# An attention and FFN kernel on Trainium2: v pieces and w3 loads in another order, one product in the short chunk

## Chip, core and metric

The kernel runs on one core of a Trainium2 chip. The metric is device time in microseconds (us) of one execution. Five runs of the kernel before gave a median of 572.65 us (571.81 to 573.43). A core has five engines with a queue of instructions each: TensorE (PE in the profile, with PEld for its weight loads), VectorE (DVE), ScalarE (ACT), GpSimd (POOL) and SyncE (SP). They run side by side and wait for each other through semaphores; each queue runs in order. SP issues the stores of the output and the transposes by DMA, POOL issues the loads.

## What is computed

```python
B, N, C = (4, 5824, 256)
qn = q / (np.linalg.norm(q, axis=1, keepdims=True) + 1e-06)
kn = k / (np.linalg.norm(k, axis=1, keepdims=True) + 1e-06)
s = kn.transpose(0, 2, 1) @ qn / tau
s = s - s.max(-1, keepdims=True)
a = np.exp(s)
a /= a.sum(-1, keepdims=True) + 1e-09
x = (v @ a).reshape(B * N, C)
out = ((x @ w1) * (x @ w2) @ w3) @ w_out     # w1, w2: 256 x 1024, w3: 1024 x 1024, w_out: 1024 x 256
```

All inputs and the output are float32. The attention is over the 256 columns (a is 256 x 256 for each of the 4 batches), then an FFN multiplies two projections and projects the product back.

## The kernel before

**Folding.** For each batch the 256 x 256 matrix a is multiplied into w1 and w2 first, which gives `Wf` (the folds, L342 to L387). Also w3 and w_out are multiplied once, into `W_sb` (`w_unit`, L624). What is left for each row block is `a = vT x Wf[0]`, `b = vT x Wf[1]`, their product, and that times `W_sb`.

**Tiling.** A batch has 5824 rows: 45 groups of 128 and 64 left over. `v` is loaded in six pieces of up to eight groups (`PIECE`), cast to bf16 on the way, and transposed into `vT` (slots of 128 rows) and, for the last full group with the 64 left over, `vTt`. A chunk is four slots, 512 columns; there are eleven of them and a short chunk of 128 + 64 columns (`NCH` is 12). A piece serves two chunks: piece 1 serves chunks 2 and 3, piece 3 chunks 6 and 7. Pieces, chunks and batches are counted from 0 in all that follows; the fourth and fifth v piece are pieces 3 and 4.

**The main loop** (L694) goes over batches, chunks and eight blocks j of 128 columns of F. `emit_ab` (L457) issues two products for `a` and two for `b`, a copy of `a` to SBUF on ACT (L469) and the product with `b` on DVE (L478; for the short chunk L480, and L483 for the 64 left over). The result waits in the list `pend`; `emit_out` (L488) multiplies it with `W_sb` and, at j = 7, copies the finished tile (ACT L524, DVE L525) and stores it (SP L526). `LAG` results are kept waiting; until `W_sb` is ready none is taken out, and afterwards up to two at each step. The 64 rows left over of an even and the following odd batch make up one 128-row product together (`lefts`).

**What sets the order.** The program is issued in a written order, not by a scheduler. `make_agenda` (L644) fills a list of due times on a running count of the time that PE's products should take (`clock`); `run_due` issues what is due between the steps of the main loop. On the agenda stand the loads of the next pieces (`moves`), their transposes 4 later, the score products of the next batch (`score_units`, between `t0` and `t1`) and its softmax and folds (`soft_units`).

**Queues.** POOL's queue holds the loads, and what stops them from starting early: `gate` (L448, a copy of one element that waits for the latest product) and `hold` (L453, a copy of one element that waits for the transposed piece before). The all-reduce of the norms (L258) is in the same queue. SP's queue holds the transposes by DMA and the output's stores.

**The start.** Batch 0's q and k come first, then v piece 0, w1 and w2, v pieces 1 and 2, w_out and w3 (L601, L602). Piece 0 and piece 1 are transposed on PE in halves (`transpose_half_on_pe`), piece 2 and all that follow by DMA on SP. w3 is transposed by four DMAs (L553) into buffers of k's pool; `w_unit` then makes `W_sb` in eight parts, each of eight products. Batch 0's sums of the exponentials (L328) are taken by products with a column of ones; DVE adds 1e-9 and takes the reciprocal `rs` (L334, L335), by which the folds are scaled.

Of the kernel before, what the change touches and what calls it, by code (L numbers as in the profile page):

```python
# [12 lines left out]
F32 = DT.float32  # L13
BF16 = DT.bfloat16

P = 128
PIECE = 8
LAG = 2
IN_BUFS = {"q": 5, "k": 6, "v": 3}
MM_COL = 1.0 / 2400.0  # L20
MM_FIX = 0.0025
# [3 lines left out]
def kernel(  # L25
# [52 lines left out]
    nc.vector.memset(warm, 0.0)  # L78
    ones_pp = consts.tile([P, P], F32)
    nc.vector.memset(ones_pp, 1.0)  # L80
    eps_t = consts.tile([P, 1], F32)
    nc.vector.memset(eps_t, 1e-6)

# [65 lines left out]
    def transpose_piece(n, pi):  # L149
        if pi == 0:  # L150
            new_vT(n)
        vT, vTt = vTs[n]
        t = pieces.pop(("v", n, pi))
        if pi < NP_ - 1:
            nc.sync.dma_start_transpose(vT[:, pi * PIECE : (pi + 1) * PIECE, :, :], t[:, :, :])
        else:
            g = LAST - 1
            nc.sync.dma_start_transpose(vT[:, pi * PIECE : pi * PIECE + g, :, :], t[:, :g, :])
            nc.sync.dma_start_transpose(vTt[:, :, :P], t[:, g, :])
            nc.sync.dma_start_transpose(vTt[:, :, P:], t[:LEFT, g + 1, :])  # L160


    G_tiles = {}
# [75 lines left out]
    def soft_units(n):  # L239
# [75 lines left out]
        def exps(ct):  # L315
# [3 lines left out]
                out=st["e"][:, ct, :], in_=st["s"][:, ct, :], func=AF.Exp, scale=st["r"][:, ct : ct + 1]  # L319
            )  # L320

        def sum_mm(c2):
            if c2 == 0:
                st["sum"] = psum.tile([P, 512], F32, tag="out" if n == 0 else "G", name=f"sum_{n}", bufs=3 if n == 0 else 1)
                Wf[n] = wf_pool.tile([P, CT, 2, F], BF16, tag="Wf", name=f"Wf_{n}")
            m = st["sum"]
            for c1 in range(CT):
                nc.tensor.matmul(  # L328
                    m[:, c1 : c1 + 1], lhsT=st["e"][:, c2, c1 * P : (c1 + 1) * P], rhs=ones_b,
                    start=(c1 == 0 and c2 == 0), stop=(c1 == CT - 1 and c2 == CT - 1), skip_group_check=True,  # L330
                )
            if c2 == CT - 1:
                rs = work.tile([P, CT], F32, tag="rs", name=f"rs_{n}", bufs=2)
                nc.vector.tensor_scalar_add(rs, m[:, :CT], 1e-9)  # L334
                nc.vector.reciprocal(rs, rs)  # L335
                st["rs"] = rs

        def sums():
# [61 lines left out]
                    quarter_mm(256, c1, c2)  # L400

        if n == 0:
            return [k_first, k_row, q_first, scaled_first, first_folds, second_quarter] + [lambda i=i: fold(i) for i in range(4, 8)]

        return (
            [(0.0, 0.0, norms), (0.0, 6.0, k_row)]
# [50 lines left out]
    def emit_ab(b, c, j):  # L457
        n = chunk_cols(c)
        tiles = []
        for w in range(2):  # L460
            t = psum.tile([P, 512], F32, tag="ab", name=f"{'ab'[w]}_{b}_{c}_{j}", bufs=4)
            for ct in range(CT):
                nc.tensor.matmul(  # L463
                    t[:, :n], lhsT=Wf[b][:, ct, w, j * P : (j + 1) * P], rhs=rhs_of(b, c, ct),
                    start=(ct == 0), stop=(ct == CT - 1),
                )
# [3 lines left out]
        if b == 0 and c < 2:  # L470

            if j % 4 == 0:
                held[0] = in_pool.tile([P, 4, 512], BF16, tag="q", name=f"abq_{c}_{j}", bufs=IN_BUFS["q"])
            ab = held[0][:, j % 4, :]
        else:
            ab = work.tile([P, 512], BF16, tag="ab_sb", name=f"abs_{b}_{c}_{j}", bufs=8 * NDEF + 6)
        if n == 4 * P:
            nc.vector.tensor_mul(ab, a_sb, tiles[1])  # L478
        else:
            nc.vector.tensor_mul(ab[:, :P], a_sb[:, :P], tiles[1][:, :P])  # L480
            if b % 2 == 0 and j == 0:
                lefts[b // 2] = work.tile([P, FT, 2, LEFT], BF16, tag="left", name=f"left_{b}", bufs=1)
            nc.vector.tensor_mul(lefts[b // 2][:, j, b % 2, :], a_sb[:, P:n], tiles[1][:, P:n])  # L483
        pend.append((b, c, j, ab))
        last_ab[0] = ab
        clock[0] += 4 * (n * MM_COL + MM_FIX)

    def emit_out(b, c, j, ab):  # L488
        small = c == NCH - 1
        if small:  # L490
            lhs = [ab[:, :P]]
            if b % 2 == 1:
                lhs.append(lefts[b // 2][:, j, :, :].rearrange("p b t -> p (b t)"))
        else:
            lhs = [ab[:, i * P : (i + 1) * P] for i in range(4)]
        if j == 0:
# [2 lines left out]
                for h in range(len(lhs) if small else 2)  # L499
            ]  # L500
        tl = out_tiles[b, c]
        for s, lhsT in enumerate(lhs):
            h, o = (s, 0) if small else divmod(s, 2)
            nc.tensor.matmul(  # L504
                tl[h][:, o, :], lhsT=lhsT, rhs=W_sb[:, j, :],
                start=(j == 0 and o == 0), stop=(j == FT - 1 and (small or o == 1)),
                skip_group_check=True,
            )
# [89 lines left out]
    load_part("v", 0, 0, half, PIECE)  # L598
    load_piece("v", 0, 1)
    load_piece("v", 0, 2)  # L600
    nc.gpsimd.dma_start(out=wout_sb, in_=moe_w_out.rearrange("(lh ll) c -> ll lh c", ll=P))  # L601
    nc.gpsimd.dma_start(out=w3_bf, in_=w3r)  # L602
    squares("k", 4, whole)
    for sl in (lo, hi):
        squares("q", 4, sl)
# [4 lines left out]
    for i, sl in enumerate(parts):  # L610
# [5 lines left out]
        if i == 0:  # L616
            soft0[1]()
    soft0[3]()
    busy(3)
    transpose_half_on_pe(0, 0, 0, False)  # L620
    soft0[4]()
    w_ready = [False]

    def w_unit(jt):  # L624
        m = psum.tile([P, 512], F32, tag="ab", name=f"w_{jt}", bufs=4)
        for lt in range(FT):
            nc.tensor.matmul(  # L627
                m[:, :D], lhsT=w3T[jt // 2][:, jt % 2, lt, :], rhs=wout_sb[:, lt, :],
                start=(lt == 0), stop=(lt == FT - 1),
            )  # L630
        if jt % 2 == 0:
            nc.scalar.copy(W_sb[:, jt, :], m[:, :D])
        else:
            nc.vector.tensor_copy(W_sb[:, jt, :], m[:, :D])
        if jt == FT - 1:
            w_ready[0] = True

    def load_library():

# [4 lines left out]
    def make_agenda(b):  # L644
# [3 lines left out]
        if b == 0:  # L648
            at(0.5, 0.87, soft0[5])
            for i in range(4):  # L650
                at((1.7, 2.6, 3.5, 3.9)[i], 0.43, soft0[6 + i])
# [38 lines left out]
        for i, (cst, t, fn) in enumerate(soft):  # L690
            at(t1 + 1.0 + t + (2.0 if b == 0 and i > 0 else 0.0), cst, fn)
        agenda.sort()

    for b in range(B):  # L694
        make_agenda(b)
        for c in range(NCH):
            for j in range(FT):
                run_due()
                emit_ab(b, c, j)
                npop = 0  # L700
                while w_ready[0] and len(pend) > LAG and npop < 2:
                    emit_out(*pend.pop(0))
                    npop += 1
                    run_due()
# [38 lines left out]
```

## Time and profile before

| What | us |
|---|---|
| median of five runs | 572.65 (571.81 to 573.43) |
| the profiled execution | 573.43 |
| its span, first to last instruction | 571.4 |
| first a product on PE | 37.94 |
| w_out issued, us to landing | 36.3, 15.1 |
| w3 issued, us to landing | 37.2, 24.0 |
| first and last w product on PE | 65.4, 76.1 |
| PE's longest wait after the start, for w3T | 0.71 |
| last PE product ends | 567.73 |

The span is the time from the first to the last instruction; the profiled execution's own time holds 2.0 us more around it. A line of a timeline gives start and duration in us, engine, source line, operation and tiles, `out<-in`, and in brackets the idle time ahead with what ended it. In a line of waits the numbers are the total, the count and the longest. In the lines of the DMA issues the last number is the time from the issue to the landing. The granted clock of TensorE was 1.00 throughout the work.

### The profile page before, as it was taken

What the parts mean: (1) busy time and instruction counts of PE and PEld (TensorE: products, weight loads), DVE (VectorE), ACT (ScalarE), POOL (GpSimd) and SP (SyncE); (2) the same over time, 40 slices, a digit from 0 to 9 for tenths busy, and PEclk for the clock granted to TensorE, in tenths of its full rate; (3) what the DMA queues carried; (4) which work ended last, traced back from release to release, by engine and by line L of the source; (5) the groups of instructions that cost most, each with busy time, mean ns of one, the idle gap of its engine ahead of it and who ended that gap; (6) DMA issues with size and microseconds to landing.
All of it is one profiled execution on the core that took longest, in us unless ns stands there. A gap on an engine that the chain in (4) does not pass through costs nothing.

```text
span 571.4 us, 10131 instructions
## 1 busy us (share of the span) xinstructions
PE 558.4 (98%) x3753; PEld 354.8 (62%) x3753; DVE 377.5 (66%) x613; ACT 339.7 (59%) x627; POOL 78.3 (14%) x164
## 2 busy tenths in 40 slices
PE   7789999999999999999999999999999999999997
PEld 5664567776655666666666666666665666666665
DVE  1047645788967567888767567787877656565564
ACT  1047535778756577777665577777765554454454
POOL 4260012112030110120220011021120000000000
PEclk9999999999999999999999999999999999999999
DMA  9999988897674596686761595856750325221011
GB/s 211 212 168 209 158 164 203 206 207 173 149 170 103 101 216 147 114 157 153 148 148 46 122 199 134 154 119 125 178 117 38 84 73 148 63 63 75 38 68 61
DMA packets 75104, 77.45 MB, mean 136 GB/s; under 512 B 54192, under 2 KB 58800, under 8 KB 75056
## 3 DMA queue, kind: packets, MB, share of 16 engines
q0 software_dynamic: 15760, 38.93, 39.4%
q1 hardware_dynamic: 59072, 37.69, 21.6%
q8 instruction: 29, 0.48, 0.3%
q10 hardware_dynamic: 224, 0.20, 0.1%
q14 instruction: 19, 0.16, 0.1%
HBM read 78.91 MB, written 23.86 MB: 180 GB/s over the span
## 4 chain that ended last, share of the span: by engine, by line
PE 91%; DMA 6%; ACT 1%; DVE 1%; issue 0%; POOL 0%; ACTq 0%; POOLq 0%
PE o L504 27%; PE a L463 27%; PE b L463 27%; PE G L188 5%; DMA k<-in_k_dram 5%; PE fold L350 2%; DMA w3T<-w_wout 1%; PE w L627 1%; ACT as L469 1%; PE quarter L376 0%; ACT kr L279 0%; POOL k L109 0%; DVE s L313 0%; ACT e L318 0%; DVE abs L478 0%
## 5 line engine op out<-in xcount | busy, mean ns | idle before, releaser
L478 DVE TENSOR_TENSOR abs<-as,b 128x512 bf16<-128x512 bf16 x336 | 230.0, 686 | 140.3 <-ACT as L469 127.8
L469 ACT CAST as<-a 128x512 bf16<-128x512 f32 (+1 forms) x384 | 215.9, 563 | 172.7 <-DVE abs L478 85.0
L463 PEld LDWEIGHTS <-Wf 128*128 128x128 bf16 x1536 | 149.0, 98 | 102.8 <-issue 2.3
L463 PE MATMUL a<-vT,Wf 128*128 128x512 bf16 x704 | 209.4, 379 | 0.8 <-DVE Wf L387 0.6
L504 PE MATMUL o<-W_sb,abs 128*128 128x256 bf16 x1376 | 209.9, 273 | 0.1
L463 PE MATMUL b<-vT,Wf 128*128 128x512 bf16 x704 | 209.3, 379 | 0.0
L504 PEld LDWEIGHTS <-abs 128*128 128x128 bf16 x1376 | 134.5, 98 | 81.9 <-DVE abs L480 0.3
L197 DVE TENSOR_TENSOR acc<-acc,sq 128x1024 f32<-128x1024 f32 x66 | 80.4, 1218 | 0.4 <-ACT sq L185 0.4
L188 PE MATMUL G<-k,q 128*128 128x256 bf16 x276 | 49.6, 273 | 0.0
L185 ACT ACTIVATE sq<-q 128x512 f32<-128x512 bf16 x66 | 41.8, 634 | 0.0
L185 ACT ACTIVATE sq<-k 128x512 f32<-128x512 bf16 x66 | 41.5, 629 | 0.0
L451 POOL COPY gate_t<-abs 1x1 bf16<-1x1 bf16 x39 | 10.5, 269 | 170.9 <-DVE abs L478 170.0
L525 DVE COPY osb<-o 128x512 f32<-128x512 f32 x44 | 30.1, 683 | 0.8 <-PE o L504 0.7
L188 PEld LDWEIGHTS <-q 128*128 128x128 bf16 x276 | 27.0, 98 | 3.1
L524 ACT COPY osb<-o 128x512 f32<-128x512 f32 x44 | 25.8, 586 | 3.8 <-PE o L504 1.8
L455 POOL COPY gate_t<-vT 1x1 bf16<-1x1 bf16 x17 | 3.3, 195 | 178.1 <-DMA vT<-v 178.1
L109 POOL DMA_DIRECT2D q<-in_q_dram x28 | 15.2, 541 | 13.1 <-DMA k<-in_k_dram 5.5
L279 ACT ACTIVATE kr<-row 128x256 f32<-128x256 f32 x1 | 0.4, 384 | 26.2 <-PE row L267 26.2
L357 ACT ACTIVATE Wf<-fold,rs 128x512 bf16<-128x512 f32 x15 | 10.3, 688 | 8.9 <-PE fold L350 7.7
L350 PE MATMUL fold<-w,e 128*128 128x512 bf16 x56 | 15.0, 379 | 0.2 <-ACT as L469 0.2
L478 DVE TENSOR_TENSOR abq<-as,b 128x512 bf16<-128x512 bf16 x16 | 10.8, 686 | 5.2 <-ACT as L469 4.6
L109 POOL DMA_DIRECT2D k<-in_k_dram x24 | 13.6, 566 | 4.1 <-DMA k<-in_k_dram 3.3
(95 smaller groups left out, 234.3 us busy)
## 6 DMA issues: line engine op xcount, KB each, us to landing
out_dram<-osb SPq DMA_DIRECT2D x44, 512.0 KB, 3.1
k<-in_k_dram POOLq DMA_DIRECT2D x19, 512.0 KB, 8.6
v<-in_v_dram POOLq DMA_DIRECT2D x19, 512.0 KB, 5.3
q<-in_q_dram POOLq DMA_DIRECT2D x18, 512.0 KB, 5.8
w_wout<-in_moe_w_dram POOLq DMA_DIRECT2D x1, 2048.0 KB, 24.0
k<-in_k_dram POOLq DMA_DIRECT2D x4, 320.0 KB, 5.9
v<-in_v_dram POOLq DMA_DIRECT2D x4, 320.0 KB, 5.2
q<-in_q_dram POOLq DMA_DIRECT2D x3, 320.0 KB, 4.3
```

What stands on the lines that cost most here:

```text
L109: nc.gpsimd.dma_start(out=pieces[nm, n, pi][:, lo:hi, :], in_=qk_main[nm, n][0][:, pi * PIECE + lo : pi * PIECE + hi, :])
L185: nc.scalar.activation(out=dst[:, :, part, :], in_=src[:, o : o + 2, :], func=AF.Square)
L188: nc.tensor.matmul(G[:, ct, :], lhsT=qt[:, i, ct * P : (ct + 1) * P], rhs=kt[:, i, :], start=(pr == 0 and part == 0 and ct == 0), stop=(pr ...
L197: nc.vector.tensor_add(accs[n], accs[n], sqs[0])
L350: nc.tensor.matmul(m, lhsT=st["e"][:, c2, c1 * P : (c1 + 1) * P], rhs=w12[:, c2, w, lo:hi], start=(c2 == 0), stop=(c2 == CT - 1),)
L451: nc.gpsimd.tensor_copy(gate_t, last_ab[0][:1, :1])
L463: nc.tensor.matmul(t[:, :n], lhsT=Wf[b][:, ct, w, j * P : (j + 1) * P], rhs=rhs_of(b, c, ct), start=(ct == 0), stop=(ct == CT - 1),)
L469: nc.scalar.copy(a_sb[:, :n], tiles[0][:, :n])
L478: nc.vector.tensor_mul(ab, a_sb, tiles[1])
L504: nc.tensor.matmul(tl[h][:, o, :], lhsT=lhsT, rhs=W_sb[:, j, :], start=(j == 0 and o == 0), stop=(j == FT - 1 and (small or o == 1)), skip ...
L524: nc.scalar.copy(o[:, 0:2, :], tl[0])
L525: nc.vector.tensor_copy(o[:, 2:4, :], tl[1])
```

## The change

Seven edits, all in the kernel's order and tiles:

- The second v piece (piece 1) of batch 0 is transposed by DMA on SP instead of on PE; pieces 2 and 1, in this order, are transposed before w3.
- w_out and w3 are loaded by POOL only when piece 1 has been transposed (`load_w3` behind a `hold`).
- The parts of `W_sb` are due from 35.0 instead of 26.0, in PSUM tiles of the tag `out` instead of `ab`.
- Batch 0's moves have other times. The first hold waits for the last w3T tile; v pieces 3 and 4 are loaded one behind the other without a hold between, and transposed one behind the other.
- In the short chunk DVE makes one product of 192 columns. The 64 left over lie behind the 128 for an even batch and ahead of them for an odd one, so that the two parts of 64 stand side by side.
- For batch 0 the 1e-9 comes from a product with the constant `tiny` that opens the sums' accumulation; DVE's add falls away.
- `LAG_END` keeps five results waiting in the last chunk; the softmax of batch 1 is no longer due 2.0 later than in the other batches.

```diff
+LAG_END = 5
@@
+    tiny = consts.tile([1, P], F32)
+    nc.vector.memset(tiny, 1e-9)
@@ transpose_piece
-            nc.sync.dma_start_transpose(vTt[:, :, :P], t[:, g, :])
-            nc.sync.dma_start_transpose(vTt[:, :, P:], t[:LEFT, g + 1, :])
+
+            first = n % 2 == 0
+            nc.sync.dma_start_transpose(vTt[:, :, :P] if first else vTt[:, :, LEFT:], t[:, g, :])
+            nc.sync.dma_start_transpose(vTt[:, :, P:] if first else vTt[:, :, :LEFT], t[:LEFT, g + 1, :])
@@ soft_units
+        def sum_start():
+            st["sum"] = psum.tile([P, 512], F32, tag="out" if n == 0 else "G", name=f"sum_{n}", bufs=3 if n == 0 else 1)
+            Wf[n] = wf_pool.tile([P, CT, 2, F], BF16, tag="Wf", name=f"Wf_{n}")
+            if n == 0:
+
+                nc.tensor.matmul(
+                    st["sum"][:, :CT], lhsT=tiny, rhs=ones_pp[:1, :CT], start=True, stop=False, skip_group_check=True
+                )
...
-                nc.vector.tensor_scalar_add(rs, m[:, :CT], 1e-9)
-                nc.vector.reciprocal(rs, rs)
+                if n > 0:
+                    nc.vector.tensor_scalar_add(rs, m[:, :CT], 1e-9)
+                nc.vector.reciprocal(rs, rs if n > 0 else m[:, :CT])
@@ emit_ab
+        if c == NCH - 1:
+            if b % 2 == 0 and j == 0:
+                lefts[b // 2] = work.tile([P, FT, 2, P + LEFT], BF16, tag="left", name=f"left_{b}", bufs=1)
+            both = lefts[b // 2][:, j, b % 2, :]
+            nc.vector.tensor_mul(both, a_sb[:, :n], tiles[1][:, :n])
+            ab = both[:, :P] if b % 2 == 0 else both[:, LEFT:]
...
-            ab = work.tile([P, 512], BF16, tag="ab_sb", name=f"abs_{b}_{c}_{j}", bufs=8 * NDEF + 6)
-        if n == 4 * P:
+                ab = work.tile([P, 512], BF16, tag="ab_sb", name=f"abs_{b}_{c}_{j}", bufs=8 * NDEF + 2)
             nc.vector.tensor_mul(ab, a_sb, tiles[1])
-        else:
-            nc.vector.tensor_mul(ab[:, :P], a_sb[:, :P], tiles[1][:, :P])
...
-            nc.vector.tensor_mul(lefts[b // 2][:, j, b % 2, :], a_sb[:, P:n], tiles[1][:, P:n])
@@ emit_out
-                lhs.append(lefts[b // 2][:, j, :, :].rearrange("p b t -> p (b t)"))
+                lhs.append(lefts[b // 2][:, j, :, :].rearrange("p b t -> p (b t)")[:, P : P + 2 * LEFT])
...
-        for s, lhsT in enumerate(lhs):
+        for s, lhsT in reversed(list(enumerate(lhs))) if small else enumerate(lhs):
@@ the start
-    nc.gpsimd.dma_start(out=wout_sb, in_=moe_w_out.rearrange("(lh ll) c -> ll lh c", ll=P))
-    nc.gpsimd.dma_start(out=w3_bf, in_=w3r)
...
+    soft0[6]()
     busy(3)
...
-        m = psum.tile([P, 512], F32, tag="ab", name=f"w_{jt}", bufs=4)
+        m = psum.tile([P, 512], F32, tag="out", name=f"w_{jt}", bufs=3)
...
+    def load_w3():
+        nc.gpsimd.dma_start(out=wout_sb, in_=moe_w_out.rearrange("(lh ll) c -> ll lh c", ll=P))
+        nc.gpsimd.dma_start(out=w3_bf, in_=w3r)
@@ make_agenda, batch 0
-            at(7.0, 0.5, lambda: transpose_half_on_pe(0, 1, 0, True))
-            at(8.0, 0.5, lambda: transpose_half_on_pe(0, 1, 1, False))
-            at(15.0, 0.0, transpose_w3)
-            at(15.0, 0.0, lambda: transpose_piece(0, 2))
+            at(0.0, 0.0, lambda: transpose_piece(0, 2))
+            at(0.0, 0.0, lambda: transpose_piece(0, 1))
+            at(0.0, 0.0, lambda: hold(vTs[0][0][:1, PIECE, 0, :1]))
+            at(0.0, 0.0, load_w3)
+            at(16.0, 0.0, transpose_w3)
             for jt in range(FT):
-                at(26.0 + 1.2 * jt, 0.87, lambda jt=jt: w_unit(jt))
-            moves = [("qk", 1, 0, 29.0), ("v", 0, 3, 30.0), ("qk", 1, 1, 43.0), ("qk", 1, 2, 47.0), ("v", 0, 4, 53.0)]
-            moves += [("qk", 1, 3, 62.0), ("qk", 1, 4, 66.0), ("v", 0, 5, 72.0), ("qk", 1, 5, 81.0)]
-            moves += [("v", 1, 0, 94.0), ("v", 1, 1, 104.0), ("v", 1, 2, 114.0), ("qk", 2, 0, 126.0)]
+                at(35.0 + 1.2 * jt, 0.87, lambda jt=jt: w_unit(jt))
+            moves = [("qk", 1, 0, 35.0), ("v", 0, 3, 35.5), ("v", 0, 4, 36.0), ("qk", 1, 1, 49.0), ("qk", 1, 2, 51.0)]
+            moves += [("qk", 1, 3, 57.0), ("qk", 1, 4, 60.0), ("v", 0, 5, 66.0), ("qk", 1, 5, 79.0)]
+            moves += [("v", 1, 0, 92.0), ("v", 1, 1, 102.0), ("v", 1, 2, 120.0), ("qk", 2, 0, 130.0)]
...
-        before = (0, 2) if b == 0 else None
+        before = "w3" if b == 0 else None
         for nm, m, pi, t in moves:
-            if before is not None:
-                at(t, 0.0, lambda w=before: hold(vTs[w[0]][1][:1, 0, :1] if w[1] == NP_ - 1 else vTs[w[0]][0][:1, w[1] * PIECE, 0, :1]))
+            if before is not None and not (nm == "v" and before == (m, pi - 1) == (0, 3)):
+                at(t, 0.0, lambda w=before: hold(w3T[-1][:1, 1, FT - 1, :1] if w == "w3" else vTs[w[0]][1][:1, 0, :1] if w[1] == NP_ - 1 else vTs[w[0]][0][:1, w[1] * PIECE, 0, :1]))
...
-            at(t1 + 1.0 + t + (2.0 if b == 0 and i > 0 else 0.0), cst, fn)
+            at(t1 + 1.0 + t, cst, fn)
@@ main loop
-                while w_ready[0] and len(pend) > LAG and npop < 2:
+                lag = LAG_END if b == B - 1 and c == NCH - 1 else LAG
+                while w_ready[0] and len(pend) > lag and npop < 2:
```

More of the change, by code (lines that the diff above doesn't have):

```diff
@@ L320, in exps @@
             )
+        def sum_start():
[5 more added lines that the diff above has]
+                )
         def sum_mm(c2):
-            if c2 == 0:
-                st["sum"] = psum.tile([P, 512], F32, tag="out" if n == 0 else "G", name=f"sum_{n}", bufs=3 if n == 0 else 1)
-                Wf[n] = wf_pool.tile([P, CT, 2, F], BF16, tag="Wf", name=f"Wf_{n}")
+            if c2 == 0 and n > 0:
+                sum_start()
             m = st["sum"]
@@ L329, in sum_mm @@
                     m[:, c1 : c1 + 1], lhsT=st["e"][:, c2, c1 * P : (c1 + 1) * P], rhs=ones_b,
-                    start=(c1 == 0 and c2 == 0), stop=(c1 == CT - 1 and c2 == CT - 1), skip_group_check=True,
+                    start=(n > 0 and c1 == 0 and c2 == 0), stop=(c1 == CT - 1 and c2 == CT - 1), skip_group_check=True,
                 )
@@ L402, in soft_units @@
         if n == 0:
-            return [k_first, k_row, q_first, scaled_first, first_folds, second_quarter] + [lambda i=i: fold(i) for i in range(4, 8)]
+            return [k_first, k_row, q_first, scaled_first, first_folds, second_quarter, sum_start] + [lambda i=i: fold(i) for i in range(4, 8)]
         return (
@@ L469, in emit_ab @@
         nc.scalar.copy(a_sb[:, :n], tiles[0][:, :n])
[L470 to L474, printed above, removed]
-        else:
-            ab = work.tile([P, 512], BF16, tag="ab_sb", name=f"abs_{b}_{c}_{j}", bufs=8 * NDEF + 6)
-        if n == 4 * P:
-            nc.vector.tensor_mul(ab, a_sb, tiles[1])
-        else:
-            nc.vector.tensor_mul(ab[:, :P], a_sb[:, :P], tiles[1][:, :P])
-            if b % 2 == 0 and j == 0:
-                lefts[b // 2] = work.tile([P, FT, 2, LEFT], BF16, tag="left", name=f"left_{b}", bufs=1)
-            nc.vector.tensor_mul(lefts[b // 2][:, j, b % 2, :], a_sb[:, P:n], tiles[1][:, P:n])
+        if c == NCH - 1:
[4 more added lines that the diff above has]
+            ab = both[:, :P] if b % 2 == 0 else both[:, LEFT:]
+        else:
+            if b == 0 and c < 2:
+                if j % 4 == 0:
+                    held[0] = in_pool.tile([P, 4, 512], BF16, tag="q", name=f"abq_{c}_{j}", bufs=IN_BUFS["q"])
+                ab = held[0][:, j % 4, :]
+            else:
+                ab = work.tile([P, 512], BF16, tag="ab_sb", name=f"abs_{b}_{c}_{j}", bufs=8 * NDEF + 2)
+            nc.vector.tensor_mul(ab, a_sb, tiles[1])
         pend.append((b, c, j, ab))
@@ L650, in make_agenda @@
             for i in range(4):
-                at((1.7, 2.6, 3.5, 3.9)[i], 0.43, soft0[6 + i])
+                at((1.7, 2.6, 3.5, 3.9)[i], 0.43, soft0[7 + i])
             at(0.0, 0.0, load_library)
             at(4.6, 0.5, lambda: transpose_half_on_pe(0, 0, 1, False))
-            at(7.0, 0.5, lambda: transpose_half_on_pe(0, 1, 0, True))
-            at(8.0, 0.5, lambda: transpose_half_on_pe(0, 1, 1, False))
-            at(15.0, 0.0, transpose_w3)
-            at(15.0, 0.0, lambda: transpose_piece(0, 2))
+            at(0.0, 0.0, lambda: transpose_piece(0, 2))
[3 more added lines that the diff above has]
+            at(16.0, 0.0, transpose_w3)
             for jt in range(FT):
-                at(26.0 + 1.2 * jt, 0.87, lambda jt=jt: w_unit(jt))
-            moves = [("qk", 1, 0, 29.0), ("v", 0, 3, 30.0), ("qk", 1, 1, 43.0), ("qk", 1, 2, 47.0), ("v", 0, 4, 53.0)]
-            moves += [("qk", 1, 3, 62.0), ("qk", 1, 4, 66.0), ("v", 0, 5, 72.0), ("qk", 1, 5, 81.0)]
-            moves += [("v", 1, 0, 94.0), ("v", 1, 1, 104.0), ("v", 1, 2, 114.0), ("qk", 2, 0, 126.0)]
+                at(35.0 + 1.2 * jt, 0.87, lambda jt=jt: w_unit(jt))
+            moves = [("qk", 1, 0, 35.0), ("v", 0, 3, 35.5), ("v", 0, 4, 36.0), ("qk", 1, 1, 49.0), ("qk", 1, 2, 51.0)]
+            moves += [("qk", 1, 3, 57.0), ("qk", 1, 4, 60.0), ("v", 0, 5, 66.0), ("qk", 1, 5, 79.0)]
+            moves += [("v", 1, 0, 92.0), ("v", 1, 1, 102.0), ("v", 1, 2, 120.0), ("qk", 2, 0, 130.0)]
             t0, t1 = 54.0, 113.0
@@ L689, in make_agenda @@
         soft = soft_units(n)
-        for i, (cst, t, fn) in enumerate(soft):
-            at(t1 + 1.0 + t + (2.0 if b == 0 and i > 0 else 0.0), cst, fn)
+        for cst, t, fn in soft:
+            at(t1 + 1.0 + t, cst, fn)
         agenda.sort()
```

## The prediction

> **What bounds the kernel now.** I read the engine totals and the chain first, then TensorE's waits, then the timelines of PE, POOL and SP between 40 and 112 us with the DMA landings beside them.
>
> ```profile
> PE 558.4 (98%) x3753; PEld 354.8 (62%) x3753; DVE 377.5 (66%) x613; ACT 339.7 (59%) x627; POOL 78.3 (14%) x164
> PE 91%; DMA 6%; ACT 1%; DVE 1%; issue 0%; POOL 0%; ACTq 0%; POOLq 0%
> ```
>
> TensorE (PE) is busy for 98% of the span and holds 91% of the chain. Work taken off DVE, ACT or POOL pays only where PE waited for it; every new wait of PE costs its full length.
>
> ```profile
> 44.95 0.59 PE L463 MATMUL b<-vT,Wf 128*128 128x512 bf16 x2
> 45.38 0.61 PE L132 MATMUL tr_I-613_614<-ident_b,v 128*128 128x128 bf16 x8
> 45.83 0.59 PE L463 MATMUL a<-vT,Wf 128*128 128x512 bf16 x2
> ...
> 64.11 0.59 PE L463 MATMUL b<-vT,Wf 128*128 128x512 bf16 x2
> 65.41 1.05 PE L627 MATMUL w<-w_wout,w3T 128*128 128x256 bf16 x8 [0.71 <-DMA w3T<-w_wout]
> ...
> 103.58 0.38 PE L188 MATMUL G<-k,q 128*128 128x256 bf16 x2
> ```
>
> In PE's timeline the distance from start to start is the price, since listed durations overlap: two 512-wide products 0.43 (44.95 to 45.38), eight transposes 0.44, one 256-wide product 0.11. A wait therefore costs more than its bracket: the b pair of 64.11 is through by 64.54, so 0.87 is lost before w at 65.41, and 0.36 likewise at 69.25, where the bracket says 0.19. Batch 0 loses 1.23 to w3T. The last row is the first G product of the pieces k and q 1 of batch 1.
>
> ```profile
> 61.30 9.52 SPq L553 DMA_TRANSPOSE w3T<-w_wout  x4
> 70.88 16.58 SPq L155 DMA_TRANSPOSE vT<-v  x2
> ```
>
> SP starts w3's four transposes when w3 has landed (issued 37.2, 24.0 to landing). They land at 65.4, 69.2, 71.0 and 72.9.
>
> ```profile
> 89.60 0.18 POOL L455 COPY gate_t<-vT 1x1 bf16<-1x1 bf16 x1 [12.23 <-DMA vT<-v]
> 89.84 0.18 POOL L451 COPY gate_t<-abs 1x1 bf16<-1x1 bf16 x1
> 90.16 0.53 POOL L109 DMA_DIRECT2D q<-in_q_dram  x1
> 90.68 0.54 POOL L109 DMA_DIRECT2D k<-in_k_dram  x1
> ```
>
> POOL holds the loads of q and k 1 until v piece 3 is transposed (89.5). The landing view of the last row alone is
>
> ```profile
> k<-in_k_dram POOLq DMA_DIRECT2D x1, 512.0 KB, 8.8
> ```
>
> so k lands at 99.5 and PE first uses it at 103.58: 4.1 of slack. This slack is what I watch.
>
> **The change, part by part.**
>
> *Second v piece by DMA.* Sixteen PE transposes go: 2 x 0.44, −0.9. Their copies on ACT (1.01) and DVE (0.68) cover nothing. SP now transposes piece 2, then piece 1. Piece 2 lands last, 35.8 + 12.9 = 48.7 (piece 1 at 45.1). A first transpose takes 4.1 to landing (w3T), the next follows 1.9 later (the last w3T at 72.9, vT behind it at 74.8): piece 1 is there at 54.7. PE comes to chunk 2 at 55.9 − 0.9 = 55.0: no wait. Bounds: 54.2, if the first takes 3.6 like the lone ones; 56.6, if the second lags 3.8 as the second w3T did, a wait of 1.6.
>
> *w_out and w3 loaded behind it.* POOL's hold waits for 54.7, and 0.4 later w_out is issued (a hold and a gate took 0.7). From an idle queue 512 KB took 5.3; w_out's pieces took 0.3 more than others in line: 60.7. w3 took 9.8 behind w_out (51.4 to 61.2): 70.5. First w3T: 0.1 + 4.1 later, 74.7. PE reaches w_0 after 44 more 512-wide products and 16 fewer transposes, counted in the two orders: 64.54 + 9.5 − 0.9 = 73.1. It waits 1.6; the old 1.23 goes: +0.3. From 54.2 the wait is 1.1 (−0.1); if the second w3T lags as before, some 0.4 more. w's PSUM tile only changes its tag. When W is ready 43 products wait for their outputs, 16 of them in q's buffers, so 34 ab_sb buffers suffice.
>
> *The first loads behind w3T.* POOL now holds q and k 0 until the last w3T. In the only series of four it lands 7.5 after the first: 82.2. The gap lies between the first and second (3.8 against 1.9 for the others); without it, 80.4. Then q 0, k 0, v 3, v 4 go out: first issue 0.8 after, the third landing 10.2 after that issue (75.6 to 85.8), the fourth 2.4 more: v 3 at 93.2, v 4 at 95.6. A transpose lands 3.7 after: v 3 at 96.9, v 4 at 99.3. PE needs v 3 for chunk 6 at 110.54 − 1.23 − 13.7 (96 256-wide outputs, 22 G products and 16 transposes fewer ahead) + 1.6 = 97.2, just in time. On SP the first stores of out stand behind both transposes; three osb buffers carry them.
>
> *The fourth and fifth piece together* is where I expect the loss. The hold ahead of q and k 1 now waits for v 4 at 99.3. Issue 0.7 later, 100.0; k 1 lands 9.3 after q's issue with a store beside it (90.2 to 99.5) or 8.0 without (112.6 to 120.6): 108.0 to 109.3. In PE's order the first G product of k 1 stands behind 28 more 512-wide products, 40 fewer outputs and 16 fewer transposes: +6.0 − 4.3 − 0.9 = +0.8. PE arrives at 103.58 − 1.23 + 0.8 + 1.6 = 104.8 and waits 3.2 to 4.5; ACT waits there too, for the square of k 1. Without the gap among w3T's landings it is 1.4 to 2.7; if v 4's load and v 3's transpose slow each other by 1.0 (no row shows such a pair), up to 5.5. I take 3.8. A later v 1 moves the arrival and the landing alike. The following loads have room: k 2 lands two loads later, some 114 to 115, and is needed at 118.
>
> *The short chunk.* Eight DVE pairs per batch (284 + 213 ns) become one product of 192 columns, about 351 by a line through 284 at 128 and 686 at 512. PE's product count is unchanged. In batch 0's end PE lost 1.0 in three waits there and just before (0.19, 0.18 and 0.17 in brackets, each 0.16 more in starts). The all-reduce of the norms also stood behind a hold of POOL until 159.85 although DVE had its input at 155.6; it now stands ahead of that hold, which is why the removed 2.0 of delay should cost nothing. I take −0.9 (bounds −1.4, with small losses, and −0.3). The other three short chunks lose some 0.6 together: −0.4.
>
> *Tail and constants.* LAG_END moves three outputs behind the last a and b: the 0.3 that PE waits for DVE at 567.3 goes, but the first pairs then queue on DVE: −0.1 (−0.4 to +0.3). The added constant product (one fp32 product of the start took 0.26) lies in PE's idle 0.77 before the sums at 36.23; the dropped add of 0.15 hides behind the quarter products, which end at 37.39, after the reciprocal. Both 0; exposed, they would be +0.3 and −0.2.
>
> Sum: −0.9 + 0.3 + 3.8 − 0.9 − 0.4 − 0.1 = +1.8. The profiled execution took 573.43 (span 571.4 and 2.0 around it) and would take 575.2; it stands 0.78 above the median of 572.65, which becomes 574.5.
>
> The warm-up products took 564 ns on average against 379 later at granted clock 1.00, so a cold TensorE is slower; after PE's longest later wait, 1.9, the rows show full speed. "TensorE: Matmul & The Clock Gate", Part 1, of the Trainium skill, says an idle window of about 3.4 us halves the clock, for at least about 3.4 us after. By it a wait of 3.8 could cost 1.7 more. No row here has such a wait, and the sum goes without it.
>
> **The rivals.**
>
> *The loads come in time: faster.* Place: k 1's landing. If w3T's series runs without its gap and k 1 needs only 8.0, it lands at 106.2, PE waits 1.4, and the gains at the chunk ends reach their upper bounds: −0.9 + 0.1 + 1.4 − 1.4 − 0.6 = −1.4, 571.3. It decides once the wait for k 1 is under about 1.6. For it: the second w3T alone shows the gap. Against: both bounds must fall well.
>
> *Gains and wait cancel: no change,* 572.6: a wait near 2, the other terms as taken.
>
> *More is late: slower still.* Piece 1 misses chunk 2 by 1.6, or the loads slow each other by 1.0 and PE restarts slower: 576.5.
>
> *It does nothing it says:* excluded for the transposes, which leave PE's order.
>
> **How the numbers follow.** Forecast 0.43, more late 0.15, cancel 0.24, faster 0.18. A measurement here tells 0.2% (1.15 us) from no change; so slower 0.58, same 0.24, faster 0.18. Range 571.4 to 576.9: from the faster case to a little over the late one. The likeliest case's own range is 573.9 to 576.
>
> **What would show it.** Right: a PE wait of 3 to 4.5 at the first G product of k 1 near 105 us, released by a DMA of k; w3T first landing at 74 to 75; no PE wait at chunk 2; the all-reduce of batch 1 before the hold on v. Wrong: k 1 landed before PE arrives, or a longer wait at chunk 2 or 6, or waits left at the end of batch 0.

## The result and the profile after

The changed kernel takes 575.82 us in the median (572.71 to 578.27 over 24 runs), the kernel before 572.55 beside it (571.31 to 575.6 over 47): ratio 1.0049, 95% interval 1.0037 to 1.0061, so slower by half a per cent. The forecast was 574.5, slower, with a range of 571.4 to 576.9. The profiled execution took 577.98, with a span of 576.2 where the one before had 571.4.

First the page of the changed kernel: the engine totals, the chain by engine, and the granted clock in 40 slices of 14.4 us.

```profile
PE 559.7 (97%) x3739; PEld 355.3 (62%) x3739; DVE 376.2 (65%) x580; ACT 339.9 (59%) x626; POOL 80.9 (14%) x164
...
PEclk9999999799999999999999999999999999999999
...
PE 86%; DMA 10%; POOL 1%; ACT 1%; issue 1%; DVE 1%; POOLq 0%; ACTq 0%
```

Fourteen product records fewer, and yet PE is busy for longer; DMA's share of the chain goes from 6% to 10%; and one slice, the eighth (101 to 115 us), has a clock below full speed. The place is in PE's timeline of that stretch (start, duration, and in brackets the idle time ahead with what ended it):

```profile
101.69 0.59 PE L477 MATMUL a<-vT,Wf 128*128 128x512 bf16 x2
102.12 0.59 PE L477 MATMUL b<-vT,Wf 128*128 128x512 bf16 x2
102.56 0.60 PE L519 MATMUL o<-W_sb,abs 128*128 128x256 bf16 x4
107.80 0.58 PE L193 MATMUL G<-k,q 128*128 128x256 bf16 x2 [4.65 <-DMA k<-in_k_dram]
108.18 1.06 PE L519 MATMUL o<-W_sb,abs 128*128 128x256 bf16 x4
109.03 0.63 PE L193 MATMUL G<-k,q 128*128 128x256 bf16 x2
109.46 1.06 PE L477 MATMUL a<-vT,Wf 128*128 128x512 bf16 x2
110.31 1.06 PE L477 MATMUL b<-vT,Wf 128*128 128x512 bf16 x2
...
113.62 0.59 PE L477 MATMUL a<-vT,Wf 128*128 128x512 bf16 x2
```

Two things are to be seen. The first G product of k 1 waits 4.65 for its load. And the products behind the wait are slow: from a at 109.46 to b at 110.31 there are 0.85, where the same distance was 0.43 before it (101.69 to 102.12). This ends at 113.6. The windows of 5 us (stretch, length, busy time of PE, PEld, DVE, ACT and POOL, granted clock, DMA share, GB/s) say so directly:

```profile
100.00:105.00 5.00, 3.15 (x23) 2.10 (x22) 3.64 (x5) 2.94 (x6) 4.08 (x9) 1.00 1.04 168
105.00:110.00 5.00, 2.20 (x10) 1.39 (x10) 0.00 (x0) 0.63 (x1) 0.00 (x0) 0.67 1.03 256
110.00:115.00 5.00, 5.00 (x25) 2.90 (x24) 1.95 (x3) 2.22 (x4) 2.07 (x3) 0.65 1.06 213
115.00:120.00 5.00, 5.00 (x39) 3.63 (x38) 5.00 (x7) 3.75 (x7) 0.00 (x0) 1.00 1.06 212
```

Between 110 and 115 PE is busy throughout and gets through 25 products instead of some 40. That is no stall and has no line in the list of waits, but it costs 2.8 us (below). In smaller windows the granted clock is still 1.00 from 103.2 to 106.6, the first 3.4 us of the idle time, and 0.50 from 106.7 to 113.5.

Why k 1 is late stands in POOL's timeline, the lines that answer to those shown of before at 89.60:

```profile
97.26 1.24 POOL L469 COPY gate_t<-vT 1x1 bf16<-1x1 bf16 x1 [15.01 <-DMA vT<-v]
98.56 0.18 POOL L465 COPY gate_t<-abs 1x1 bf16<-1x1 bf16 x1
98.80 0.53 POOL L112 DMA_DIRECT2D q<-in_q_dram  x1
99.32 0.54 POOL L112 DMA_DIRECT2D k<-in_k_dram  x1
```

The hold ends with the transpose of v 4 (landed 97.14), k 1 is issued at 99.32 instead of 90.68 and lands at 107.76. In the list of PE's waits between 60 and 135 us (in total, times, longest) there is one line:

```profile
PE G L193 <- DMA k<-in_k_dram: 4.6, 1, 4.6
```

So nothing waited at chunk 6. Nor at chunk 2, which starts at 54.7: the list over the whole span has no wait of PE for a DMA of vT. Of the end of batch 0, one wait is left where before there were three:

```profile
185.03 0.33 PE L477 MATMUL b<-vTt,Wf 128*128 128x192 bf16 x2 [0.40 <-DVE Wf L373]
```

**How lost time is counted from here on.** Brackets understate a wait, and a slow clock has none. So I laid PE's order of products, each at its distance from start to start at full clock, beside the ends in the trace; the growth of the difference over a stretch is the time lost there. "Lost starts" below are these.

### The profile page after: what moved, and what is told of

Read it like the earlier page. It is cut to its first block, busy times and chain, and to the rows that moved or that the text cites. A ratio compares the mean times of both kernels' runs of the same rounds, so it can differ in the third digit from the quotient of the medians.

```text
span 576.2 us, 10068 instructions
## 1 busy us (share of the span) xinstructions
PE 559.7 (97%) x3739; PEld 355.3 (62%) x3739; DVE 376.2 (65%) x580; ACT 339.9 (59%) x626; POOL 80.9 (14%) x164
## 4 chain that ended last, share of the span: by engine, by line
PE 86%; DMA 10%; POOL 1%; ACT 1%; issue 1%; DVE 1%; POOLq 0%; ACTq 0%
PE b L477 26%; PE o L519 26%; PE a L477 26%; PE G L193 5%; DMA k<-in_k_dram 4%; PE fold L364 2%; DMA v<-in_v_dram 2%; DMA q<-in_q_dram 2%; DMA w3T<-w_wout 1%; DMA vT<-v 1%; POOL q L112 0%; POOL k L112 0%; ACT kr L284 0%; ACT as L483 0%; PE quarter L390 0%
## 5 line engine op out<-in xcount | busy, mean ns | idle before, releaser
L519 PE MATMUL o<-W_sb,abs 128*128 128x256 bf16 x1344 | 201.4, 274 | 0.0
L519 PEld LDWEIGHTS <-abs 128*128 128x128 bf16 x1344 | 132.0, 98 | 79.1 <-issue 0.6
L469 POOL COPY gate_t<-vT 1x1 bf16<-1x1 bf16 x16 | 4.6, 289 | 142.1 <-DMA vT<-v 142.1
L488 DVE TENSOR_TENSOR left<-as,b 128x192 bf16<-128x192 bf16 x32 | 11.2, 353 | 5.4 <-ACT as L483 3.2
```

The source lines that it names most:

```text
L519: nc.tensor.matmul(tl[h][:, o, :], lhsT=lhsT, rhs=W_sb[:, j, :], start=(j == 0 and o == 0), stop=(j == FT - 1 and (small or o == 1)), skip ...
```

## The experiments

Nine of the twelve runs change one or two places of the changed kernel, or of a version made from it; three (the early pairing, the short chunk alone, the all-reduce ahead) change the kernel before.

**Is the hold the cause?** The hold ahead of q and k 1 was taken away; all else stays.

```
-            if before is not None and not (nm == "v" and before == (m, pi - 1) == (0, 3)):
+            if before is not None and not (nm == "v" and before == (m, pi - 1) == (0, 3)) and (m, pi, before) != (1, 1, (0, 4)):
```

> The changed kernel without the hold ahead of the loads of q and k 1 of batch 1, so that they follow v 4 directly. Theory (the hold on the transposed v 4 makes k 1 late): k 1 lands near 98 to 101, before TensorE comes to it at 103.0; no wait there, granted clock 1.00 throughout, and the time falls by 4.9 for the wait and by what the clock cost, to 568 to 569.5. Rival (the hold keeps loads and transposes apart, and without it they slow each other): the transpose of v 3 lands after 97 and a wait of some us appears at chunk 6; 571 to 575.

Measured: 587.71 (587.23 to 589.83), ratio 1.0279 (1.0247 to 1.0312). k 1 did land in time, at 98.58, and the kernel became slower still by 2%: my theory fell. The rival had the mechanism, transposes and loads that slow each other, but put the time at 571 to 575. The waits and SP's timeline of this run show what the hold had kept away:

```profile
PE a L477 <- DMA vT<-v: 15.0, 1, 15.0
```

```profile
91.04 19.35 SPq L158 DMA_TRANSPOSE vT<-v  x2
```

The transposes of v 3 and v 4 occupy SP's queue for 19.35 instead of 4.02. The first of them took 19.7 to land. The DMA view says why. Its lines give the packets of each queue, MB and the share of 16 engines' time; q0 carries POOL's loads, q1 what SP issues. First between 98 and 104 us, with the loads of q and k beside the transpose, then between 109.5 and 110.5, with none:

```profile
q0 software_dynamic: 323, 1.19, 97.6%
q1 hardware_dynamic: 322, 0.08, 10.0%
```

```profile
q1 hardware_dynamic: 1084, 0.27, 134.0%
```

Beside loads the two queues get the same number of packets, 323 and 322, but a load's packet holds 3.7 KB (1.19 MB by 323) and a transpose's 0.25 KB. With no load beside them, the transposes move 1084 packets in one microsecond. "DMA: Bandwidth & Descriptors", "Queues, rings and completion order", of the Trainium skill, states that a DMA engine takes turns between its queues packet by packet; these counts agree. So the hold costs a wait at k 1 and saves a longer one at v 3: without it PE loses 15.0 at chunk 6.

**Is the slow clock what the wait leaves behind?** Here PE is kept busy during the wait by products whose result nobody reads.

```
+            if n == 1 and pr == 4 and part == 0:
+                busy(22)
```

> The changed kernel with 22 products on constant data (4.7 us of TensorE time, results unused) ahead of the first G product of k 1, where TensorE waits. Theory (the idle wait lowers TensorE's clock, which costs time beyond the wait): the clock stays 1.00, products after 108 take 379 ns and not twice as long in starts, and the time is that of the changed kernel's runs at full clock, about 573.3, with little spread. Rival (products after the wait are slow because of the loads beside them): they stay slow, time 575.5 to 576.

Measured: 574.98 (574.68 to 575.59), ratio 1.0046 (1.0029 to 1.0063). No wait of PE for k 1 is left, as the filler lies there, and the window that had a clock of 0.65 now reads

```profile
110.00:115.00 5.00, 5.00 (x41) 3.71 (x39) 4.64 (x6) 3.96 (x8) 2.07 (x3) 1.00 1.07 215
```

with 41 products instead of 25. PE's last product ends at 569.24, not 571.92: 2.7 earlier, though the first G product of k 1 starts 0.1 later (107.89 for 107.80). So the slow clock is real, follows from the idle time and costs 2.8 in this pair of executions. It is not the loads beside the products, the rival: they are there in both (213 and 215 GB/s in this window). The five runs lie within 0.9 us of each other, the 24 of the changed kernel within 5.6. The time itself missed what I expected, 574.98 for 573.3, and is hardly better than the changed kernel's, each beside its own kernel before (1.0046 and 1.0049). The filler is paid in full in every run, and here it ended at 107.89, 0.6 after k 1 had landed (107.26); whether that explains the whole of it is not shown.

**Does the pairing cost anything by itself?** Two runs: the kernel before with v 4 right behind v 3, both early; and the changed kernel with v 4 apart, later. The first also leaves out the hold between v 3 and v 4, as the changed kernel does.

```
-("v", 0, 3, 30.0), ("qk", 1, 1, 43.0), ("qk", 1, 2, 47.0), ("v", 0, 4, 53.0)]
+("v", 0, 3, 30.0), ("v", 0, 4, 30.5), ("qk", 1, 1, 43.0), ("qk", 1, 2, 47.0)]
```

> The kernel before with one edit: v 4 loaded right behind v 3 and transposed with it, the hold of q and k 1 on v 4. Theory (the wait is the sum of two delays, w3's later load and the pairing; each alone fits into the slack of 4.1): k 1 lands 3 to 4 later than the 99.5 of before, at 102 to 103.5, TensorE comes at 103.6, no wait or one under 0.5; 572 to 573.5. Rival (the pairing alone makes the loss): a wait of 3 or more, 575.5 to 578.

```
-("v", 0, 3, 35.5), ("v", 0, 4, 36.0), ("qk", 1, 1, 49.0), ("qk", 1, 2, 51.0)]
+("v", 0, 3, 35.5), ("qk", 1, 1, 49.0), ("qk", 1, 2, 51.0), ("v", 0, 4, 53.0)]
```

> The changed kernel with v 4 apart again: loaded at 53 on the running count behind q and k 2, the hold of q and k 1 on v 3 only. Theory of the two delays: v 3 lands transposed at 94.6, k 1 at 103.3 to 104.6, a wait of 0.3 to 1.6 at 103.0, clock 1.00; 569 to 570.5. Rival (the late w3 alone makes the loss): a wait of 4 or more and a lowered clock, 574 to 577.

Measured: 571.89 (571.47 to 572.71), ratio 0.9993 (0.9979 to 1.0006), and 573.64 (572.5 to 577.04), ratio 1.003 (1.0012 to 1.0047). Paired but early, k 1 lands at 99.71 and nobody waits: no loss. Late but apart, k 1 lands at 103.32 and nobody waits for it, but the load further back now comes late, k 5 at 146.48:

```profile
PE G L193 <- DMA k<-in_k_dram: 2.4, 1, 2.4
```

So the wait for k 1 takes both: loads that start late (behind w3, behind the second v piece), and a hold that waits for two pieces. Pairing alone is free. The late loads alone are not: in this order they still lose 0.3%, at k 5.

**A version with the loads fitted to this, and its parts.** Three pairs of q and k go ahead of v 4; then three more runs each put one part of the change back.

```
-("v", 0, 4, 36.0), ("qk", 1, 1, 49.0), ("qk", 1, 2, 51.0)]
-("qk", 1, 3, 57.0), ("qk", 1, 4, 60.0), ("v", 0, 5, 66.0), ("qk", 1, 5, 79.0)]
+("qk", 1, 1, 49.0), ("qk", 1, 2, 51.0)]
+("qk", 1, 3, 57.0), ("v", 0, 4, 58.0), ("qk", 1, 4, 62.5), ("qk", 1, 5, 66.0), ("v", 0, 5, 72.0)]
```

> The changed kernel with v 4 apart (loaded behind q and k 3), the hold of q and k 1 on v 3, and q and k 5 loaded ahead of v 5. Theory (the whole loss is the wait for k and the lowered clock; the rest of the change is a gain of 2 to 2.5): no wait of TensorE for a DMA of k, clock 1.00, 1.5 to 2.5 below the kernel before, some 570. Rival (the rest of the change gains nothing): within 0.2% of the kernel before.

This version with the short chunk of the kernel before (two products, two tiles):

> The same with the short chunk of before: two products of DVE, 128 and 64 columns, and the old place of the 64. Theory (the single product takes the waits out of the short chunks): 0.6 to 1.3 slower than e5, waits of TensorE back near 180 us and some at the other short chunks. Rival (the place of the all-reduce and the softmax's due times did it): within 0.3 of e5.

With the tail's lag as before:

```
-LAG_END = 5
+LAG_END = 2
```

> e5 with two results kept waiting in the last chunk instead of five. Theory (the longer list takes one wait away and makes others, both traces have 6.03 from the first product of the last chunk to the end of the last output): within 0.3 of e5. Rival (it hides the last wait): 0.3 to 0.6 slower.

With the softmax delayed as before:

```
+            at(t1 + 1.0 + t + (2.0 if b == 0 and i > 0 else 0.0), cst, fn)
```

> e5 with the softmax of batch 1 due 2.0 later again. Theory (the all-reduce ahead of the hold is what matters, the 2.0 only covered for its delay): 0 to 0.4 slower, since the folds move 2.0 into the short chunk. Rival (the due times made the gain at the end of batch 0): 0.6 to 1.2 slower.

Measured: 577.54 (571.08 to 579.7), ratio 1.0061 (1.0032 to 1.009); 578.13 (577.77 to 578.9), 1.0102 (1.0088 to 1.0116); 576.01 (570.95 to 578.04), 1.0036 (1.0006 to 1.0067); 578.14 (571.06 to 579.36), 1.0081 (1.0052 to 1.011). All four were expected faster and are slower. The waits of the fitted version name the reason, first PE's list and then ACT's:

```profile
PE o L519 <- ACT osb L539: 4.5, 1, 4.5
```

```profile
ACT osb L539 <- DMA out_dram<-osb: 5.3, 1, 5.3
```

PE waits for a PSUM tile, ACT has not emptied it because none of the three osb buffers is free, and these are not free because their stores stand on SP behind a transpose:

```profile
119.73 0.52 SPq L541 DMA_DIRECT2D out_dram<-osb  x1
135.41 1.24 SPq L161 DMA_TRANSPOSE vT<-v  x1
136.70 1.24 SPq L164 DMA_TRANSPOSE vTt<-v  x1
138.03 1.19 SPq L165 DMA_TRANSPOSE vTt<-v  x1
139.32 2.11 SPq L541 DMA_DIRECT2D out_dram<-osb  x3
```

SP issues nothing from 120.3 to 135.4: v 5's transpose waits there for its load, three stores wait behind it, and the first frees its buffer at 146.89. The wait drops the clock too, to 0.50 between 145.9 and 152.5. In the profiled runs of the four it lasted 4.5, 5.2, 4.4 and 2.2, and the runs of three of them spread over 7 to 9 us (the four of the old short chunk over 1.1), so the times of these four tell nothing of the small parts; their lost starts do, further below.

**Freeing the store.** One more step on the fitted version: v 5's transpose later in SP's order.

```
-at(t + 4.0, 0.0, lambda m=m, pi=pi: transpose_piece(m, pi))
+at(t + (12.0 if (m, pi) == (0, 5) else 4.0), 0.0, lambda m=m, pi=pi: transpose_piece(m, pi))
```

> The version with fitted moves (v 4 apart, behind three pairs of q and k), with one more: the transpose of v 5 stands 8 steps later in SP's order (84 for 76). There it stood from 127.2, where v 5's load was issued, to 135.4, where it landed, ahead of three stores of out, so that ACT had no output buffer until 146.9 and PE lost 4.5 at an output product. Theory: the store wait goes, PE waits nowhere above 1 us between 60 and 170, the clock stays at 1.00 and the time falls from 577.5 to 569.8 (its runs without a dropped clock took 571.1 to 571.4, with some 2 us of the wait left in them). Rival (the store wait hides a wait for q and k 4 or 5, which share the queue with v 4 and v 5): a PE wait of 2 us or more at k 4 or k 5 near 140, 572 to 576.

Measured: 570.45 (569.83 to 571.57), ratio 0.9966 (0.9954 to 0.9979). The theory held, with 570.45 against 569.8. SP's timeline now has the stores ahead of the transpose:

```profile
118.92 1.01 SPq L541 DMA_DIRECT2D out_dram<-osb  x2
136.60 1.24 SPq L161 DMA_TRANSPOSE vT<-v  x1
```

There is no wait of PE between 60 and 170 us, the clock is 1.00, and the 12 runs lie within 1.7 us. This is the fastest kernel of the study, with the whole change in it except the pairing, and with other times for the loads.

**The change without the second v piece.** PE transposes that piece again, so w_out and w3 are loaded as early as before, and the parts of `W_sb` and the loads up to v 5 have their old due times; v 3 and v 4 stay together, at 30 and 30.5. The cut shows the main lines.

```
-            at(0.0, 0.0, lambda: transpose_piece(0, 1))
-            at(0.0, 0.0, lambda: hold(vTs[0][0][:1, PIECE, 0, :1]))
-            at(0.0, 0.0, load_w3)
+            at(7.0, 0.5, lambda: transpose_half_on_pe(0, 1, 0, True))
+            at(8.0, 0.5, lambda: transpose_half_on_pe(0, 1, 1, False))
...
-("qk", 1, 0, 35.0), ("v", 0, 3, 35.5), ("v", 0, 4, 36.0),
+("qk", 1, 0, 29.0), ("v", 0, 3, 30.0), ("v", 0, 4, 30.5),
```

> The changed kernel with one part undone: the second v piece is transposed by TensorE again, so that w_out and w3 are loaded, w3 is transposed and the first loads of batch 1 are issued where they were before; the fourth and fifth v piece stay together (at 30 and 30.5), and the short chunk, the softmax, the later loads and the tail stay as changed. Theory (the loss is the late start of the transposes behind w3, and pairing costs nothing as long as they start early): no wait of TensorE for k 1, granted clock 1.00 throughout, the early pairing's 571.9 less the 0.9 at the end of batch 0 and 0.3 in the other short chunks: 570.7. Rival (the pairing or the later loads cost something by themselves): a PE wait above 1 us appears somewhere in batch 0, 572 to 574.

Measured: 571.16 (570.35 to 572.29), ratio 0.9976 (0.9964 to 0.9988). No wait for k 1, clock 1.00: the theory held, with 570.7 expected. With the pairing kept, and the second v piece and the early order of the loads put back together, the loss turns into a gain of 0.24%.

**Where the gain at the end of batch 0 comes from.** Two runs from the kernel before: the single short-chunk product alone, and the all-reduce ahead of POOL's hold alone.

```
...
+            both = lefts[b // 2][:, j, b % 2, :]
+            nc.vector.tensor_mul(both, a_sb[:, :n], tiles[1][:, :n])
...
```

> The kernel before with one part of the change alone: one DVE product of 192 columns in the short chunk, with its tiles; softmax, loads and tail as before. Theory A, of the prediction (DVE's pairs of products made PE wait at the end of batch 0): its 1.7 us of lost starts there fall to about 0.9, the other short chunks give 0.4: 571.3 where the kernel before takes 572.3. Rival B (the order of the softmax and of the all-reduce made them): 1.4 us or more of lost starts stay at the end of batch 0, 571.9 to 572.2.

```
-("v", 1, 2, 114.0), ("qk", 2, 0, 126.0)]
+("v", 1, 2, 120.0), ("qk", 2, 0, 130.0)]
```

> The kernel before with two times changed alone, those of the loads of v 2 of batch 1 (114 to 120) and of q and k 0 of batch 2 (126 to 130), as in the changed kernel: the all-reduce of the norms of batch 1 then stands ahead of POOL's hold on v piece 1 instead of behind it. The short chunk's two products, the added 2.0 of the softmax and all else stay. Theory A (the order of the all-reduce made the losses of starts at the end of batch 0, about 1.7 us before and 0.9 after): they fall to 0.8 to 1.1 and the time to 571.3, where the kernel before takes 572.1. Theory B (the added 2.0 of the softmax made them, or only the short product and the softmax together): 1.5 us or more stay, 571.9 to 572.2.

Measured: 571.95 (571.22 to 572.86), ratio 0.9991 (0.9977 to 1.0004), and 572.35 (571.43 to 573.84), ratio 1.0002 (0.9992 to 1.0013): neither alone does anything that can be told from nothing, and theory A fell both times. In POOL's timeline of the second, the all-reduce does stand ahead of the hold,

```profile
154.44 3.24 POOL L258 PARTITION_ALL_REDUCE tot<-acc  x1 [5.46 <-DVE acc L256]
157.56 0.18 POOL L455 COPY gate_t<-vT 1x1 bf16<-1x1 bf16 x1
```

5.4 earlier than in the kernel before (159.85; 1.3 of it because DVE's input was there earlier, at 154.3 for 155.6), and PE lost the same time. Lost starts from the tenth chunk of batch 0 to the first of batch 1, in us, of all versions that tell the parts apart:

| version | one product | all-reduce ahead | softmax not delayed | lost |
|---|---|---|---|---|
| kernel before | no | no | no | 1.69 |
| short chunk alone | yes | no | no | 1.64 |
| all-reduce ahead alone | no | yes | no | 1.69 |
| fitted, old short chunk | no | yes | yes | 1.06 |
| fitted, softmax delayed | yes | yes | no | 1.02 |
| changed kernel | yes | yes | yes | 0.78 |

With the all-reduce ahead, either of the other two brings 0.6 to 0.7, and both bring 0.9. Each of two parts of the three was tried alone and gives 0.05 at most. The softmax without its delay was not tried alone, nor with the all-reduce behind the hold; and the rows named fitted have later loads than the first three, so that 0.1 more or less there is not told apart. The version without the second v piece has all three parts and loads as early as the first three rows, and loses 0.8: the early loads do not change the picture.

## Why the prediction was right, and where it was not

The sign and the mechanism were right: the pair's late transposes hold the load of k 1, and PE waits for it at the first G product of k 1. The total was near for a reason that is partly luck: the medians differ by 3.3, where the sum had 1.8, and the profiled executions by 4.5. The terms, for the profiled executions:

| term of the sum | predicted | measured |
|---|---|---|
| sixteen PE transposes gone | -0.9 | -0.9 |
| waits for w3T | +0.3 | -1.1 |
| wait for k 1 | +3.8 | +4.8 |
| half clock behind it | left out | +2.8 |
| end of batch 0 | -0.9 | -0.9 |
| other short chunks and tail | -0.5 | -0.2 |
| sum | +1.8 | +4.5 |

The measured column is in lost starts, but for the first row, which is the predicted price of the products that are gone. PE's last product moved by 4.19, from 567.73 to 571.92, so the terms overstate it by 0.3: the first a product starts 0.2 earlier (37.76 for 37.94), and a loss of 0.1 just ahead of chunk 2 is gone. The end of the span lies 4.3 behind that product instead of 3.6; the difference of 0.6 has no cause shown here.

**w3T, the step with the wrong sign.** I had the last of the early v pieces, piece 2, loaded at 48.7; it landed at 47.10. All behind it came 1.4 to 1.8 earlier: the second piece was transposed by 52.86 (sum: 54.7), w3 landed at 69.11 (70.5) and the first w3T at 72.96 (74.7). PE came to it at 72.8, near the 73.1 of the sum, and lost 0.18 there instead of the predicted 1.6, against 1.24 before. The 48.7 was the row of one execution, a late one: in all other profiled executions, where these loads stand in the same place, piece 2 landed at 46.3 to 47.5. So was the old 1.24: the early pairing and the short chunk alone, which load w3 as the kernel before does, lost nothing there in theirs. The new 0.18 is no firmer, as other versions with the second piece by DMA lost from nothing to 1.0. For the release of the loads I had taken 7.5 for the series of four from the one series there was, with its gap between the first and the second. The series after has none: first and last landed at 72.96 and 79.01, 6.05 apart.

**The wait for k 1, a term mis-sized by 1.0.** PE arrived at 103.0, not 104.8: it had not lost the 1.4 at w3T, and 0.4 more was gone. The load gained less. w3T's last landing came 3.2 before the 82.2 of the prediction, v 4's transpose 2.2 before its 99.3, the issue of q 1 only 1.2 before its 100.0 (the hold's copy took 1.24 instead of the 0.18 it took before), and k 1 landed 9.0 after that, at 107.76, 0.8 before the 108.6 that a wait of 3.8 meant. Two mis-sized terms that depend on each other nearly cancel: +0.3 and +3.8 make 4.1, -1.1 and 4.8 make 3.7.

**The clock, the step that failed.** The sum left out any loss of clock, since no row of the kernel before had such a wait. The page that I had cited, "TensorE: Matmul & The Clock Gate", Part 1, was right: an idle window of about 3.4 us halves the clock. Here an idle time of 4.65 was followed by products at double distance until 113.5, a loss of 2.8 where I had priced 1.7 apart from the sum. In the fitted version an idle time of 4.45 did the same, but with the tail's lag as before one of 4.4 left the clock at 0.50 only from 146.3 to 149.6 and cost 1.4: the length of the slow stretch is not fixed by the wait. The 2.4 at k 5 in the version with v 4 apart left the profiled clock at 1.00, though four of its ten runs had a mean of 0.994 to 0.997. The runs of the changed kernel show the mixture: four of 25 had a mean clock of 1.00 and took 572.71 to 574.84; seven with 0.989 to 0.993 took 576.72 to 578.27; the others lie mostly between. A mean of 0.996 to 0.998 alone says little, as runs of the kernel before have it too and are no longer (572.14 with 0.996). The median of 575.82 is one point in that spread, so 574.5 was near it without the term that makes the spread.

**The end of batch 0, right in size, and not by the part named first.** The sum had -0.9 for the single product together with the all-reduce, and "the removed 2.0 of delay should cost nothing". Measured, 1.69 fell to 0.78. But the product alone gives 0.05 and the all-reduce alone nothing; the removed delay, given no price, is worth 0.2 of it when the two others are there, and 0.6 with the all-reduce alone. The DVE product itself was as estimated, 353 ns for 351.

**The other short chunks and the tail.** They lose 1.22 before and 1.00 after (0.25 to 0.18, 0.35 to 0.21, 0.62 to 0.61): 0.2 instead of 0.4. LAG_END gains nothing: the fitted version loses 0.61 in the last two chunks with 5, and 0.55 with 2. I had predicted -0.1 within -0.4 and +0.3.

**Of its own signs,** two of those named for right came: no wait at chunk 2, and the all-reduce ahead of the hold (162.02 and 165.14). Two missed in number: the wait's bracket was 4.65 for 3 to 4.5, and the first w3T landed at 72.96 for 74 to 75. One named for wrong came too, a wait left at the end of batch 0: the 0.40 for a Wf that DVE writes.

**Of the rivals,** the one that has the loads in time gave 571.3. Two versions of the study are that case: with the loads early or the store freed, 571.16 and 570.45. "More is late" was closest to the profiled execution in what it named, a slow restart of PE, though not in its place at chunk 2: no wait of PE there.

## What to carry

Work that is moved from PE to a queue is priced by the order behind it: here 0.9 saved on PE put a hold and a load in another order, the next arrangement delayed three stores, and with the transposes on SP a gain appeared only when each of these had its slot. An idle time of PE of 4.4 to 4.65 cost its length and 1.4 to 2.8 more in the profiled executions, so find the load with the least slack and give it a place ahead of whatever waits for a transpose. When one queue carries both transposes and stores, a transpose that waits for its load blocks the stores behind it, and through their buffers the engine that does no DMA at all (4.5 us of PE here).

## What the runs showed of the hardware, unexpected

A DMA transpose beside loads did not get half of the bandwidth but half of the packets: 322 packets of 0.25 KB to 323 of 3.7 KB, and 19.7 us to landing against 3.7 for one alone (90.27 to 93.96 in the fastest version). A hold that looks like lost time for the loads was what kept it short. And the 24 runs of a kernel with one wait of 4.65 lay 5.6 us apart, while the five with that idle time filled lay 0.9 apart. The spread alone is no proof of the clock, as 47 runs of the kernel before, which has no such wait, lay 4.3 apart; the granted clock beside each run tells.
